# Spreading the tokens of experts 5 to 8 by transfers in SBUF and turning them on VectorE

## The chip, the core and the metric

One core of a Trainium2 chip runs the kernel. The core's engines work side by side, each through its own queue in order: PE (TensorE, matrix products), DVE (VectorE), ACT (ScalarE), POOL (GpSimd) and SP (SyncE, which here issues transfers). Products land in PSUM, from where DVE and ACT read them; everything else lies in SBUF. The metric is the device time of one execution in microseconds (us); lower is better, and a run is told by the median of its executions.

## The reference

Three stages follow each other. An attention stage makes 4352 tokens of 512 features, a dense layer with a softplus works on them, and then every token is given to one of eight experts, 544 tokens to each (`cap`), by the order of the gate's logits. The change touches only the last stage:

```python
def _moe2_ref(x, w_gate, w1, w2):
    ...
    out = np.zeros((N, D), dtype=np.float32)
    for e in range(E):
        mask = assigned == e
        h = np.maximum(x[mask] @ w1[e], 0.0)
        out[mask] = h @ w2[e]
    return out.astype(np.float32)
```

`x[mask]` is 544x512, `w1[e]` 512x1024, `w2[e]` 1024x512, all float32.

## The kernel before

All products of this stage are made from split operands: a value is kept as a high part (`hi`, rounded for the fast float32 product) and a low part (`lo`, the rest), and three products stand for one.

The loop over `ph` (line 1245) runs through the eight experts, `ph` 0 to 7, which the text calls experts 1 to 8. Each has two phases on PE. The **first phase** (line 1277) is 16 units of 12 products: `w1h`/`w1l` times the turned tokens `yTh`/`yTl`, a unit being one of eight slices of 128 hidden features by one of two parts of the tokens (`HALF`). From expert 2 on, the units begin with the part of tokens 256 to 543, which are pieces 2, 3 and 4, and take tokens 0 to 255, pieces 0 and 1, in the second unit. The **second phase** is a short block for the last 32 tokens (line 1308) and four blocks of 24 products (line 1322), for `a` = 2, 3, 0, 1. ACT copies the result of each block to `ot` (lines 1311 and 1328), and POOL scatters it to DRAM.

Between the matmuls of the second phase the next expert is prepared. `prepare` (line 1193) is a generator that is advanced 16 times, after every six products of the four blocks; each advance splits one eighth of `w1` (ACT copy, POOL difference, line 1158) and, when its condition holds, turns one piece of the tokens. `transposes` (line 1177) turns a piece of up to 128 tokens: four PE transposes of 128x128 into one PSUM bank `p_h` (of two), an ACT copy to `yTh` (line 1189), a DVE difference to `yTl` (line 1190). The tokens come to `xg` by five indirect gathers on POOL (line 1133). `load_w1` and `load_w2` bring the weights by one transfer of 2 MB each on SP.

Through the whole stage a third job runs in small steps at fixed places between the matmuls (`advance_route`, at the product numbers in `AT1`, `AT2` and `AT3`): it finds which tokens the next experts take. It is a chain that goes back and forth between DVE (lines 1019 to 1103) and short products on PE (lines 1044, 1061, 1072, 935, 940). It ends in the first phase of expert 6, so that the starts of experts 7 and 8 have none of it.

The order of the instructions on each engine is the order in which the program writes them; nothing reorders it later.

Of the kernel before, what the change touches and what calls it, by code (L numbers as in the profile page):

```python
# [8 lines left out]
F32 = mybir.dt.float32  # L9
# [21 lines left out]
def attn_moe_kernel(ctx, tc, x_s, x_t, state_t, w_in, w_out, w_gate, w1, w2, out):  # L31
    nc = tc.nc
    V, A, G, PE, SP = nc.vector, nc.scalar, nc.gpsimd, nc.tensor, nc.sync
# [7 lines left out]
    def bank(tag, bufs=1):  # L41
        return psum.tile([128, 512], F32, name="p_" + tag, tag=tag, bufs=bufs)
# [1062 lines left out]
    W1S, W2S, XG, W1, YT = {}, {}, {}, {}, {}  # L1105
    regs, gathered, unit = {}, {}, [0]

    def expert_reg(ph):
        if ph not in regs:
            regs[ph] = SP.value_load(RES[ph][0][0:1, 0:1], min_val=0, max_val=E - 1)  # L1110
        return regs[ph]

    def load_w1(ph):
        t = ldp.tile([128, 4, F2], F32, name="s1w")
        SP.dma_start(t, w1[bass.ds(expert_reg(ph), 1)].rearrange("o (k p) f -> p (o k) f", p=128))
        W1S[ph] = t

    def load_w2(ph):
        t = ldp.tile([128, 8, DM], F32, name="s2w")
        if ph == 0:  # L1120

            G.memset(t[0:1, 0, 0:1], 0.0)
        SP.dma_start(t, w2[bass.ds(expert_reg(ph), 1)].rearrange("o (k p) f -> p (o k) f", p=128))
        W2S[ph] = t

    def gather(ph, some=range(5)):
        idx = RES[ph][1]
        if 0 in some:
            XG[ph] = ldp.tile([128, 5, DM], F32, name="xg")
        xg = XG[ph]  # L1130
        for a in some:
            m = 128 if a < 4 else CAP - 512
            G.indirect_dma_start(out=xg[0:m, a, :], out_offset=None, in_=y_d[:, :],
                                 in_offset=bass.IndirectOffsetOnAxis(ap=idx[0:m, a:a + 1], axis=0))
        gathered[ph] = unit[0]

    def routing():
# [7 lines left out]
    for i, at_ in enumerate(route(0, False)):  # L1145
        if lazy and i % 2 == 0:
            lazy.pop(0)()
        rest(99 if at_ == "slots" else BETWEEN[i])
        if 0 in RES and 0 not in W1S:
            load_w1(0)  # L1150
# [4 lines left out]
    me = ctx.enter_context(tc.tile_pool(name="me", bufs=1))  # L1155
# [5 lines left out]
    def split_w1(ph, on=(G,)):  # L1161
        src = W1S.pop(ph)
        hi = w1p.tile([128, 4, F2], F32R, name="w1h")
        lo = w1p.tile([128, 4, F2], F32R, name="w1l")
        W1[ph] = (hi, lo)
        for i in range(8):
            c = slice(i * 128, (i + 1) * 128)
            split_piece(src[:, :, c], hi[:, :, c], lo[:, :, c], on[0])
            yield
# [7 lines left out]
    def transposes(ph):  # L1177
        xg = XG.pop(ph)
        hi = me.tile([128, 4, CAP], F32R, name="yTh")
        lo = me.tile([128, 4, CAP], F32R, name="yTl")  # L1180
        YT[ph] = (hi, lo)
        for a in range(5):
            m = 128 if a < 4 else CAP - 512
            p = bank("h", 2)
            for k in range(4):
                PE.transpose(p[:, k * m:(k + 1) * m], xg[0:m, a, k * 128:(k + 1) * 128], ident[0:m, 0:m])  # L1186
            src = p[:, 0:4 * m].rearrange("p (k c) -> p k c", k=4)
            c = slice(a * 128, a * 128 + m)
            A.activation(hi[:, :, c], src, AF.Copy)
            V.tensor_tensor(lo[:, :, c], src, hi[:, :, c].bitcast(F32), op=OP.subtract)  # L1190
            yield

    def prepare(ph):
        sp1, tr = split_w1(ph), transposes(ph)
        n = 0
        while True:
            a, b = next(sp1, 0), 1
            if unit[0] >= gathered[ph] + 12 or n > 8:
                b = next(tr, 0)
            n += 1  # L1200
            if a == 0 and b == 0:
                return
            yield
# [22 lines left out]
    W2_FROM = 5  # L1226
    on = [G]
    sp1, tr0 = split_w1(0, on), transposes(0)

    def begin(ops):  # L1230
        for op in ops:
            if op in "sv":
                on[0] = G if op == "s" else V
                next(sp1, 0)
            elif op == "t":
                next(tr0, 0)
            elif op == "r":
                advance_route()
            elif op == "x":
                gather(0, range(2))  # L1240
            else:
                gather(0, range(2, 5))
                load_w2(0)
    begin(BEGIN)
    for ph in range(E):
# [9 lines left out]
        def fetch():  # L1255
            q = ph + 1
            if q in RES and q not in W1S and q not in W1:
                load_w1(q)
            if q in RES and ph not in W2S and q not in W2S and sp2 is None:
                load_w2(q)  # L1260
            if len(RES.get(q, ())) == 2 and q not in XG and q not in YT:
                gather(q)

        evac = lambda: None
        for u in range(16):
            ft, hf = units[u] if ph else units0[u]
            f, c = slice(ft * 128, (ft + 1) * 128), HALF[hf]
            w = c.stop - c.start
            p = bank("h", 2) if u % 2 else bank("y2" if u % 4 else "y3")
            n = 0  # L1270
# [26 lines left out]
        for a in (4, 2, 3, 0, 1):  # L1297
            ot = me.tile([128, DM], F32, name="ot", bufs=3)
            p = bank(f"y{a % 2}" if a < 4 else "y1")
            if a == 4:  # L1300

                m, ws = TAIL, W2S.pop(ph)
                evac()
                for ft in range(8):
                    if ft in AT3:
                        advance_route()
                    for q in range(4):
                        PE.matmul(p[q * 32:(q + 1) * 32, 0:128], h2t[:, ft], ws[:, ft, q * 128:(q + 1) * 128],
                                  start=(ft == 0), stop=(ft == 7))
                for q in range(4):  # L1310
                    A.activation(ot[0:m, q * 128:(q + 1) * 128], p[q * 32:(q + 1) * 32, 0:128], AF.Copy)
                fetch()
            else:
                m = 128
                c = slice(a * 128, a * 128 + m)
                n = 0
                for ft in range(8):
                    fetch()
                    for l, r in ((h2h, w2h), (h2h, w2l), (h2l, w2h)):
                        if n in AT2:  # L1320
                            advance_route()
                        PE.matmul(p, l[:, ft, c], r[:, ft, :], start=(n == 0), stop=(n == 23))  # L1322
                        n += 1
                    if ft % 2 == 1:
                        if pre is None and ph + 1 in XG and ph + 1 in W1S:
                            pre = prepare(ph + 1)
                        advance(pre)
                A.activation(ot, p, AF.Copy)  # L1328
# [6 lines left out]
        if ph + 1 < E:  # L1335
            while ph + 1 not in YT or pre is None:
                advance_route()
                fetch()
                if pre is None and ph + 1 in XG and ph + 1 in W1S:
                    pre = prepare(ph + 1)  # L1340
                advance(pre)
            while advance(pre):
                pass
# [40 lines left out]
```

## Time and profile before

| | us |
|---|---|
| median of 3 runs | 1209.81 |
| lowest and highest run | 1209.26, 1211.1 |
| the profiled execution, its own time | 1206.22 |
| its span in the trace | 1204.4 |
| first unit of experts 5, 6, 7, 8 begins on PE at | 985.63, 1042.59, 1096.67, 1147.11 |

The profiled execution is 3.6 us under the median, and 1.8 us of its own time lie outside its span. The engines' busy shares are means over stages that differ; what a change in the last stage is worth is read from that stage. In the timeline every row is one or more instructions: start, duration, engine, line, operation, names and shape, count, and in brackets how long the engine had been idle before and what it waited for.

### The profile page before, as it was taken

What the parts mean: (1) busy time and instruction counts of PE and PEld (TensorE: products, weight loads), DVE (VectorE), ACT (ScalarE), POOL (GpSimd) and SP (SyncE); (2) the same over time, 40 slices, a digit from 0 to 9 for tenths busy, and PEclk for the clock granted to TensorE, in tenths of its full rate; (3) what the DMA queues carried; (4) which work ended last, traced back from release to release, by engine and by line L of the source; (5) the groups of instructions that cost most, each with busy time, mean ns of one, the idle gap of its engine ahead of it and who ended that gap; (6) DMA issues with size and microseconds to landing.
All of it is one profiled execution on the core that took longest, in us unless ns stands there. A gap on an engine that the chain in (4) does not pass through costs nothing.

```text
span 1204.4 us, 21169 instructions
## 1 busy us (share of the span) xinstructions
PE 1148.3 (95%) x8256; PEld 905.3 (75%) x8256; DVE 649.8 (54%) x1744; ACT 640.6 (53%) x1277; POOL 484.4 (40%) x472
## 2 busy tenths in 40 slices
PE   4798999999999999999999997999999999999996
PEld 1566677777677777777777765979797988889895
DVE  6998435463363533634434266776685767641120
ACT  3776666666676666766766732533333333343330
POOL 0333423232232232322344435645646555556531
PEclk9998999999999999999999999899999999999999
DMA  7454021111201201012000003250523425234201
GB/s 245 141 193 142 1 71 36 54 53 36 70 1 42 64 29 55 23 36 70 1 18 19 1 18 123 91 197 25 200 82 143 136 80 180 106 119 133 92 18 38
DMA packets 51060, 95.77 MB, mean 80 GB/s; under 512 B 4624, under 2 KB 19088, under 8 KB 50960
## 3 DMA queue, kind: packets, MB, share of 16 engines
q1 hardware_dynamic: 45232, 76.46, 19.4%
q0 software_dynamic: 5632, 17.83, 4.4%
q8 instruction: 65, 1.06, 0.4%
q14 instruction: 35, 0.29, 0.1%
q10 hardware_dynamic: 96, 0.13, 0.0%
HBM read 76.58 MB, written 17.83 MB: 78 GB/s over the span
## 4 chain that ended last, share of the span: by engine, by line
PE 79%; DVE 10%; issue 6%; POOL 2%; ACT 1%; DMA 1%; SPq 0%; POOLq 0%; DVEq 0%; ACTq 0%
PE p_h L491 13%; PE p_y L1322 12%; PE p_y L575 8%; PE p_y L577 8%; PE p_y L579 8%; PE p_y L1277 7%; PE p_h L1277 6%; PE p_bg L460 2%; PE p_y L582 2%; PE p_bg L502 2%; PE p_y L586 2%; PE p_y L584 2%; PE p_h L1186 1%; DVE c_a L198 1%; PE p_bg L1044 1%
## 5 line engine op out<-in xcount | busy, mean ns | idle before, releaser
L557 POOL TENSOR_TENSOR g_lo<-g,g_hi 128x512 fp32r<-128x512 f32 x127 | 164.1, 1293 | 324.6 <-ACT g_hi L554 268.1
L575 PE MATMUL p_y<-g_hi,wo_hi 128*128 128x512 f32 x448 | 185.6, 414 | 0.0
L577 PE MATMUL p_y<-g_hi,wo_lo 128*128 128x512 f32 x448 | 178.3, 398 | 3.6 <-POOL wo_lo L237 3.6
L579 PE MATMUL p_y<-g_lo,wo_hi 128*128 128x512 f32 x448 | 176.4, 394 | 0.0
L554 ACT ACTIVATE g_hi<-g 128x512 fp32r<-128x512 f32 x126 | 79.6, 632 | 118.5 <-DVE g L546 84.7
L546 DVE SCALAR_TENSOR_TENSOR g<-p_h,t_sp 128x512 f32<-128x512 f32 x128 | 87.5, 684 | 98.1 <-ACT t_sp L534 97.6
L575 PEld LDWEIGHTS p_y<-g_hi,wo_hi 128*128 128x128 f32 x448 | 85.1, 190 | 49.1 <-ACT t_sp L526 12.6
L1322 PE MATMUL p_y<-w2h,h2h 128*128 128x512 f32 x256 | 105.0, 410 | 0.0
L491 PE MATMUL p_h<-at_hi,P_hi 128*128 128x512 f32 x256 | 103.6, 405 | 1.4 <-DVE g L546 1.4
L491 PE MATMUL p_h<-at_hi,P_lo 128*128 128x512 f32 x256 | 101.6, 397 | 0.0
L491 PE MATMUL p_h<-at_lo,P_hi 128*128 128x512 f32 x256 | 101.5, 397 | 0.0
L1322 PE MATMUL p_y<-w2l,h2h 128*128 128x512 f32 x256 | 101.4, 396 | 0.0
L1322 PE MATMUL p_y<-w2h,h2l 128*128 128x512 f32 x256 | 101.2, 395 | 0.0
L577 PEld LDWEIGHTS p_y<-g_hi,wo_lo 128*128 128x128 f32 x448 | 85.3, 191 | 20.7 <-POOL wo_lo L237 4.9
L579 PEld LDWEIGHTS p_y<-g_lo,wo_hi 128*128 128x128 f32 x448 | 85.3, 190 | 19.4
L1330 POOL DMA_INDIRECT out_dram<-ot,idx x40 | 38.7, 969 | 143.8 <-ACT ot L1328 72.5
L526 ACT ACTIVATE t_sp<-p_h 128x512 f32<-128x512 f32 x128 | 75.4, 589 | 27.8 <-PE p_h L491 27.0
L1159 POOL TENSOR_TENSOR w2l<-s2w,w2h 128x512 fp32r<-128x512 f32 x64 | 81.6, 1291 | 13.1 <-ACT w2h L1158 12.3
L534 ACT ACTIVATE t_sp<-t_sp 128x512 f32<-128x512 f32 x128 | 80.9, 632 | 4.1
L1159 POOL TENSOR_TENSOR w1l<-s1w,w1h 128x512 fp32r<-128x512 f32 x63 | 80.1, 1297 | 6.0 <-ACT w1h L1158 5.2
L533 ACT ACTIVATE t_sp<-t_sp 128x512 f32<-128x512 f32 x128 | 80.7, 631 | 2.3
L1277 PE MATMUL p_y<-yTl,w1h 128*128 128x288 f32 (+1 forms) x256 | 77.3, 302 | 0.0
(282 smaller groups left out, 2611.0 us busy)
## 6 DMA issues: line engine op xcount, KB each, us to landing
s1w<-in_moe_w_dram SPq DMA_DIRECT2D x8, 2048.0 KB, 8.3
s2w<-in_moe_w_dram SPq DMA_DIRECT2D x8, 2048.0 KB, 9.1
st<-in_moe_w_in_dram SPq DMA_DIRECT2D x16, 512.0 KB, 4.1
xT<-in_x_t_dram SPq DMA_DIRECT2D x16, 512.0 KB, 4.4
st<-in_moe_w_out_dram SPq DMA_DIRECT2D x16, 512.0 KB, 3.8
xt<-in_x_s_dram SPq DMA_DIRECT2D x8, 1024.0 KB, 5.5
y_d<-yz SPq DMA_DIRECT2D x48, 128.0 KB, 3.5
y_d<-s_g SPq DMA_DIRECT2D x8, 128.0 KB, 2.5
```

The costliest lines, as they stand in the source:

```text
L491: PE.matmul(h, l[:, f0:f0 + 128], r[:, par, :], start=(n == 0), stop=(n == 5))
L533: A.activation(t, t, AF.Exp, scale=-1.0)
L534: A.activation(t, t, AF.Ln, bias=1.0)
L546: V.scalar_tensor_tensor(g[:, :w], hps.pop(s)[:, :w], 0.0, tsp.pop(s)[:, :w], op0=OP.max, op1=OP.add)
L554: A.activation(hi[:, c], g[:, c], AF.Copy)
L557: (G if on[1] == "G" else V).tensor_tensor(lo[:, c], g[:, c], hi[:, c].bitcast(F32), op=OP.subtract)
L575: PE.matmul(yb[j], wo_hi[:, ft, c], hi, start=st, stop=False)
L577: PE.matmul(yb[j], wo_lo[:, ft, c], hi, start=False, stop=False)
L579: PE.matmul(yb[j], wo_hi[:, ft, c], lo, start=False, stop=sp)
L1159: eng.tensor_tensor(lo, src, hi.bitcast(F32), op=OP.subtract)
L1277: PE.matmul(p[:, :w], l[:, k, f], r[:, k, c], start=(n == 0), stop=(n == 11))
L1322: PE.matmul(p, l[:, ft, c], r[:, ft, :], start=(n == 0), stop=(n == 23))
```

## The change

For experts 5 to 8 (`ph` from `TURNED` = 4 on) the tokens are no longer turned on PE. After the gather, 16 transfers on SP copy `xg` to a new tile `xz`, in pieces of 512 bytes, so that each partition block of 32 holds one quarter of the features of 32 tokens at a time. One DVE instruction per piece (`V.transpose`, which turns 32x32 blocks) then writes the turned piece to the PSUM bank that the four PE transposes filled before. The ACT copy and the DVE difference stay. The features come out in another order, so `w1` is loaded in that order, in four transfers of 32 partitions. The pieces are made in the order 2, 3, 4, 0, 1, and a turn is tried only from the advance with `n` above 12: three of the 16 advances, all in the block `a` = 1, the others after the last of them.

```diff
+    TURNED = 4
     def load_w1(ph):
         t = ldp.tile([128, 4, F2], F32, name="s1w")
-        SP.dma_start(t, w1[bass.ds(expert_reg(ph), 1)].rearrange("o (k p) f -> p (o k) f", p=128))
+        src = w1[bass.ds(expert_reg(ph), 1)]
+        if ph < TURNED:
+            SP.dma_start(t, src.rearrange("o (k p) f -> p (o k) f", p=128))
+        else:
+            for q in range(4):
+                SP.dma_start(t[q * 32:(q + 1) * 32], src[:, q * 128:(q + 1) * 128].rearrange("o (k c) f -> c (o k) f", c=32))
...
+        if ph >= TURNED:
+            xz = me.tile([128, 17, 128], F32, name="xz")
+            for a in range(4):
+                n = 5 if a == 0 else 4
+                for q in range(4):
+                    SP.dma_start(xz[q * 32:(q + 1) * 32, a::4], xg[a * 32:(a + 1) * 32, 0:n, q * 128:(q + 1) * 128])
+            XG[ph] = xz
         gathered[ph] = unit[0]
...
-        for a in range(5):
+        for a in (range(5) if ph < TURNED else (2, 3, 4, 0, 1)):
             m = 128 if a < 4 else CAP - 512
             p = bank("h", 2)
-            for k in range(4):
+            if ph >= TURNED:
+                V.transpose(p[:, 0:4 * m].rearrange("p (k t r) -> p t k r", k=4, r=32),
+                            xg[:, 4 * a:4 * a + m // 32].rearrange("p t (k c) -> p t k c", k=4))
+            for k in range(4 if ph < TURNED else 0):
                 PE.transpose(p[:, k * m:(k + 1) * m], xg[0:m, a, k * 128:(k + 1) * 128], ident[0:m, 0:m])
...
-            if unit[0] >= gathered[ph] + 12 or n > 8:
+            if unit[0] >= gathered[ph] + 12 and ph < TURNED or n > (8 if ph < TURNED else 12):
                 b = next(tr, 0)
```

On DVE, at the end of expert 4's second phase, the queue before holds only the chain of the routing (`pe`, `sat`, `df`, `mk`), and then the first results of expert 5 (`h2l`):

```order
L1039 SCALAR_TENSOR_TENSOR p_bg_6890<-df,p_bg_6890 128x1
L1049 SCALAR_TENSOR_TENSOR pe<-p_bg_10607,rem_6897 15x8
L1051 SCALAR_TENSOR_TENSOR pe<-p_bg_10607,pe 15x8 x2
L1052 TENSOR_TENSOR sat_6910<-p_bg_10607,pe 15x8
L1058 TENSOR_TENSOR p_bg_6890<-pat,p_bg_6890 128x16
L1063 TENSOR_REDUCE df<-p_bg_10630 128x1
L1026 SCALAR_TENSOR_TENSOR p_bg_6890<-df,p_bg_6890 128x16
L1031 TENSOR_TENSOR mk_6906<-v,p_bg_6890 128x34x16
```

In the changed kernel the same stretch of DVE's queue, from the first turn to the last, reads (the rows from L1026 to L1039 stand between `df` and the third turn in both):

```order
L1202 STREAM_TRANSPOSE p_h<-xz 128x4x4x32
L1209 TENSOR_TENSOR yTl<-p_h,yTh 128x4x128
L1049 SCALAR_TENSOR_TENSOR pe<-p_bg_10596,rem_6897 15x8
L1051 SCALAR_TENSOR_TENSOR pe<-p_bg_10596,pe 15x8 x2
L1052 TENSOR_TENSOR sat_6910<-p_bg_10596,pe 15x8
L1058 TENSOR_TENSOR p_bg_6890<-pat,p_bg_6890 128x16
L1202 STREAM_TRANSPOSE p_h<-xz 128x4x4x32
L1209 TENSOR_TENSOR yTl<-p_h,yTh 128x4x128
L1063 TENSOR_REDUCE df<-p_bg_10623 128x1
```

Two turns came in between the steps of the chain. A little further on DVE, after the chain's next `mk`, stand the other three:

```order
L1039 SCALAR_TENSOR_TENSOR p_bg_6890<-df,p_bg_6890 128x1
L1202 STREAM_TRANSPOSE p_h<-xz 128x128
L1209 TENSOR_TENSOR yTl<-p_h,yTh 128x4x32
L1202 STREAM_TRANSPOSE p_h<-xz 128x4x4x32
L1209 TENSOR_TENSOR yTl<-p_h,yTh 128x4x128
L1202 STREAM_TRANSPOSE p_h<-xz 128x4x4x32
L1209 TENSOR_TENSOR yTl<-p_h,yTh 128x4x128
```

Ten instructions came in, a turn and a difference for each piece, and the differences that stood in the blocks `a` = 2 and 3 before are now here.

On ACT, the same place before, from the copy of block `a` = 0 over that of block `a` = 1 to expert 5's first result:

```order
L1328 ACTIVATE ot<-p_y_10519 128x512
L1328 ACTIVATE ot<-p_y_10587 128x512
L1158 ACTIVATE w2h<-s2w 128x512
L1282 ACTIVATE h2h<-p_y_10652 128x256
L1158 ACTIVATE w2h<-s2w 128x512
```

And now:

```order
L1347 ACTIVATE ot<-p_y_10502 128x512
L1208 ACTIVATE yTh<-p_h 128x4x128 x2
L1208 ACTIVATE yTh<-p_h 128x4x32
L1347 ACTIVATE ot<-p_y_10570 128x512
L1208 ACTIVATE yTh<-p_h 128x4x128 x2
L1174 ACTIVATE w2h<-s2w 128x512
L1301 ACTIVATE h2h<-p_y_10657 128x256
```

The five copies to `yTh` moved from the blocks `a` = 2 and 3 to here: three behind the copy of block `a` = 0, two behind that of block `a` = 1.

## Rows read from the trace of the kernel before

**Rows 1.** Page: busy time of each engine, share of the span, instructions.

```profile
PE 1148.3 (95%) x8256; PEld 905.3 (75%) x8256; DVE 649.8 (54%) x1744; ACT 640.6 (53%) x1277; POOL 484.4 (40%) x472
```

**Rows 2.** Timeline, ACT: first and last copy of experts 7 and 8's second phases.

```profile
1122.77 1.11 ACT L1311 ACTIVATE ot<-p_y 32x128 f32<-32x128 f32 x4 [1.58 <-PE p_y L1308]
...
1147.19 0.60 ACT L1328 ACTIVATE ot<-p_y 128x512 f32<-128x512 f32 x1 [4.84 <-PE p_y L1322]
...
1173.20 1.11 ACT L1311 ACTIVATE ot<-p_y 32x128 f32<-32x128 f32 x4 [1.58 <-PE p_y L1308]
...
1195.16 0.60 ACT L1328 ACTIVATE ot<-p_y 128x512 f32<-128x512 f32 x1 [4.84 <-PE p_y L1322]
```

**Rows 3.** Groups by line: busy us, mean ns of one, idle before.

```profile
L1186 PE MATMUL p_h<-ident,xg 128*128 128x128 f32 (+1 forms) x160 | 24.1, 275 | 3.3 <-DMA xg<-y_d,idx 3.3
L284 DVE TENSOR_TENSOR Z<-Z,m 128x512 f32<-128x512 f32 x12 | 14.9, 1245 | 0.4
```

**Rows 4.** One tile's or line's instructions: least, median, greatest ns.

```profile
L282 DVE STREAM_TRANSPOSE Z<-ST x12: 700/701/703, 188.2 to 566.1; 128x512 f32<-128x512 f32 x12
L1189 ACT ACTIVATE yTh<-p_h x40: 277/598/602, 752.5 to 1131.9; 128x512 fp32r<-128x512 f32 x32, 128x128 fp32r<-128x128 f32 x8
L1190 DVE TENSOR_TENSOR yTl<-p_h,yTh x40: 291/691/693, 753.1 to 1132.3; 128x512 fp32r<-128x512 f32 x32, 128x128 fp32r<-128x128 f32 x8
```

**Rows 5.** Timeline at the start of expert 5, DVE and PE.

```profile
981.60 0.17 DVE L1039 SCALAR_TENSOR_TENSOR p_bg<-df,p_bg 128x1 int32<-128x1 int32 x1
...
982.86 0.17 DVE L1049 SCALAR_TENSOR_TENSOR pe<-p_bg,rem 15x8 f32<-15x8 f32 x1 [1.09 <-PE p_bg L1044]
...
983.53 0.15 DVE L1058 TENSOR_TENSOR p_bg<-pat,p_bg 128x16 int32<-128x16 int32 x1
...
984.58 0.17 DVE L1063 TENSOR_REDUCE df<-p_bg 128x1 f32<-128x8 f32 x1 [0.90 <-PE p_bg L1061]
...
985.63 0.30 PE L1277 MATMUL p_y<-yTh,w1h 128*128 128x288 f32 x1
...
986.19 0.16 DVE L1039 SCALAR_TENSOR_TENSOR p_bg<-df,p_bg 128x1 int32<-128x1 int32 x1
...
987.55 0.27 PE L1277 MATMUL p_h<-yTh,w1h 128*128 128x256 f32 x1
```

**Rows 6.** Timeline at the start of expert 6, DVE and PE.

```profile
1039.49 0.17 DVE L1063 TENSOR_REDUCE df<-p_bg 128x1 f32<-128x8 f32 x1 [0.28 <-PE p_bg L1061]
...
1041.55 0.17 DVE L1073 TENSOR_SCALAR p_bg<-p_bg 128x8 f32<-128x8 f32 x1 [1.44 <-PE p_bg L1072]
...
1042.59 0.29 PE L1277 MATMUL p_y<-yTh,w1h 128*128 128x288 f32 x1
...
1043.29 0.24 DVE L1087 SCALAR_TENSOR_TENSOR M<-cu,em,p_bg 128x34 bf16<-128x34 f32 x1
...
1044.47 0.36 PE L1277 MATMUL p_h<-yTh,w1h 128*128 128x256 f32 x1
```

**Rows 7.** Timeline, ACT, at the start of expert 7.

```profile
1096.75 0.60 ACT L1328 ACTIVATE ot<-p_y 128x512 f32<-128x512 f32 x1 [4.84 <-PE p_y L1322]
```

**Rows 8.** Chain that ended last (start us, us): expert 7's first unit.

```profile
1096.67 1.60 PE p_y L1277 x12
```

**Rows 9.** Timeline, PE: a wait of PE between two matmuls.

```profile
114.41 0.80 PE L577 MATMUL p_y<-g_hi,wo_lo 128*128 128x512 f32 x1 [2.15 <-POOL wo_lo L237]
```

**Rows 10.** Two stretches: length, busy us by engine, granted clock, DMA share, GB/s.

```profile
112.00:116.00 4.00, 1.85 (x6) 1.30 (x5) 3.96 (x8) 2.64 (x6) 3.60 (x2) 0.80 0.86 290
116.00:120.00 4.00, 4.00 (x18) 3.22 (x17) 2.80 (x6) 0.95 (x3) 0.00 (x0) 0.77 0.03 10
```

**Rows 11.** Transfers: issues, KB each, median us from issue to landing.

```profile
y_d<-yz SPq DMA_DIRECT2D x48, 128.0 KB, 3.5
xg<-y_d,idx POOLq DMA_INDIRECT x40, 3.8
```

**Rows 12.** Timeline, POOL: the last of expert 5's five gathers.

```profile
957.48 0.88 POOL L1133 DMA_INDIRECT xg<-y_d,idx  x1 [0.30 <-issue]
```

## The prediction

> **What bounds the kernel now.** I read the page's busy times first: TensorE is busy for 95% of the span [rows 1]. Then the timeline at the starts of experts 5 to 8: the first unit follows the last block of the expert before without a wait, and the second unit follows the first [rows 5, 6, 8]. So in this stage PE ends last everywhere, work taken from its stream is worth its full length, and any new wait at a start costs its full length too. The chain that ended last says the same: a whole unit of expert 7 stands on it as twelve matmuls in a row [rows 8].
>
> **What the change removes.** Four PE transposes per piece, 20 per expert, 80 in all, and they lie in PE's stream. Their price is read from two second phases that differ in nothing else: expert 7's holds the transposes for expert 8, expert 8's holds none, and neither has a routing step. From the first copy behind the short block to the copy of the last block it is 1147.19 - 1122.77 = 24.42 us with them and 1195.16 - 1173.20 = 21.96 us without [rows 2]. So 2.46 us per expert, 0.49 us per group of four, and 4 x 2.46 = **9.8 us gained**. PE's routing waits in these phases are short, so experts 5 and 6 get the same value.
>
> The transposes' own mean duration is 275 ns [rows 3], which would make 80 of them 22 us; but four of them overlap, as the 0.49 us shows, and the step counts. The Trainium skill (VectorE: DVE Perf Modes, "The three transpose paths" and "Rules for kernel authors") speaks against this change: for a 128x128 transpose it says to use TensorE where PSUM is a good place for the result, at 390 ns against 311 ns on VectorE (bf16). By its 390 ns the sum would gain 31 us in place of 9.8 and end near 1204; the step of 0.12 us in this trace disagrees with that figure, and agrees with the rule.
>
> **What it adds, off the path.** 16 transfers per expert of some 68 KB in 512-byte pieces. SP sends them when the gather is in: for expert 5 the last gather ends at 958.4 and lands some 3.8 us later [rows 11, 12], so they start near 962. A transfer of 128 KB in 512-byte pieces lands in 3.5 us [rows 11]; even one after another 16 take under 56 us, but they are queued together and hold 1.1 MB, 9 of those 128 KB. I take 10 to 15 us, to 977 at the latest; the first turn comes near 982, so nothing waits. Behind them on SP stands only the load of `w2` of the same expert, which is needed after 986 and took 9 us; `w1` in four transfers has 25 us to spare. I cost both at nothing; if that cover failed at expert 5, each us of lateness there would be a us of the time.
>
> **What it adds, on the path.** A turn of 128x512 takes 0.70 us on DVE, the ACT copy 0.60, the DVE difference 0.69; the short piece some 0.3 for each [rows 4]. Into PSUM no row shows a turn: the ends are 0.60 (ACT over the same 512 columns) and 1.25 (the slowest two-operand DVE operation of this size [rows 3]); I take 0.70, as DVE's reads of PSUM cost 0.69. For each hand-over between engines I allow 0.05 us. What decides is the order. On DVE a difference waits for its ACT copy, and the next turn stands behind that difference: a piece is 0.70 + 0.60 + 0.69 and three hand-overs, about 2.1 us, with no overlap between pieces. On ACT the copies of pieces 2, 3 and 4 stand behind the copy of block `a` = 0, those of 0 and 1 behind that of block `a` = 1, which waits for PE's last product. Before, all this lay 25 us earlier.
>
> *Start of expert 5*, times from PE's old start 985.63 [rows 5]. DVE is through with L1039 at -3.9. Piece 2: turn to -3.1, copy to -2.5, difference to -1.7. Then the routing's L1049 to L1058 (0.82 us from 982.86 to 983.68), which used to run at -2.8; `sat` comes at -1.0, where PE's L1061 wants it by -1.2: PE is 0.3 late. Piece 3: -0.9 to 1.2. Then L1063 to L1039 (984.58 to 986.35, 1.8 us) to 3.0. Piece 4: turn 3.3, copy 3.6, difference 3.95, and only then has the first unit its operands: PE stands still from 0.3 to 3.6 and has its second matmul at 4.0. Piece 0: 4.0 to 6.1. Piece 1: turn 6.8, copy 7.45, difference 8.2. The second unit, which began at 987.55 (+1.9), gets going at 8.2 where it had its second matmul at 2.0: **6.2 us late**.
>
> *Start of expert 6*, from 1042.59 [rows 6]. DVE is free at 1039.21, -3.4 (the row's 0.28 us of idling). Piece 2 to -1.3. L1063 and the two short ones behind it, 0.6, to -0.7; PE's L1072, which ran by -1.2, waits for them, about 1.0. Piece 3 to 1.5. L1073 to L1087 (1041.55 to 1043.53, 2.0 us) to 3.5. Piece 4 to 4.45, piece 0 to 6.6, piece 1 to 8.7. Behind that stands the routing's `tot`, for which PE's L940 waits ahead of the second unit: 9.05 in place of +1.88: **7.2 us late**.
>
> *Starts of experts 7 and 8* have no routing. ACT is through with block `a` = 0 at -4.8 (4.84 us of idling ahead of the row at 1096.75, [rows 7]), the first turn is long done, and pieces 2, 3 and 4 end at -0.3: the first unit doesn't wait. ACT copies block `a` = 1 from 0.1 to 0.7. Piece 0: copy 1.3, difference 2.05. Piece 1: turn 2.75, copy 3.4, difference 4.15. The second unit is due at 1.6 [rows 8] and has its second matmul at 4.2 in place of 1.7: **2.5 us late**, twice.
>
> Together 6.2 + 7.2 + 2.5 + 2.5 = **18.4 us lost**.
>
> **The clock.** After a wait of 2.15 us PE's granted clock fell: its mean was 0.80 and then 0.77 in two stretches of 4 us, parts of which ran at 1.2 in place of 2.4 GHz [rows 9, 10]. That is 4 x 0.20 + 4 x 0.23 = 1.7 us of work lost, behind the wait and on top of it. Two other waits, of 1.87 and 2.13 us, show the same pattern. The new waits are of this kind: 3.3 us and again 1.7 us at experts 5 and 6, 2.5 us at 7 and 8 broken by one matmul. Four falls at 1.7 are **6.9 us**; the ends are 0 and, with a second fall at experts 5 and 6, 10.3.
>
> **The sum.** 18.4 + 6.9 - 9.8 = +15.5 us. The profiled execution would go from 1206.2 to 1221.7; the median of the runs stands 3.6 above it, and 1209.8 + 15.5 = **1225**. A turn of 0.60 takes off 12 x 0.1 (twelve serial turns: four each at experts 5 and 6, two each at 7 and 8) = 1.2; one of 1.25 adds 12 x 0.55 = 6.6. The forecast's own range is 1220 to 1230.
>
> **Rivals.**
> - *Waits without the clock*: the waits are cut by single units and the clock stays at 2.4 GHz. 1209.8 + 18.4 - 9.8 = 1218. For it: at experts 7 and 8 one matmul breaks the wait. Against: the three waits of about 2 us in this trace that were all followed by 1.2 GHz.
> - *Turns slow or transfers late*: a turn into PSUM costs 1.25 us, or the transfers for expert 5 come after 982. 1225 + 6.6 = 1232. For it: no row shows such a turn, and the transfers of 32 partitions are new. Against: reads of PSUM cost no more than those of SBUF here, and there are some 5 us to spare.
> - *Faster: the waits stay under what PE saves.* PE gains 2.46 us per expert; if the last piece is done that soon after the first unit, the change wins. This mechanism sits at experts 7 and 8, where 2.5 late against 2.46 is already even, and would have to hold at 5 and 6 too; with no wait at all it gives 1209.8 - 9.8 = 1200. It decides at 9.8 us of waits in all, with the clock held. For it: DVE does little besides in experts 7 and 8. Against: the order on DVE and ACT is fixed, and the chain for pieces 0 and 1 alone is 3.5 us behind ACT's last copy.
> - *The transposes are worth their durations* (22 us, by 275 ns each): 1209.8 + 25.3 - 22 = 1213. Against: the two second phases above, which differ by 2.46 us and not by 5.5.
>
> **Chances.** Forecast 0.50, waits without the clock 0.22, slow turns or late transfers 0.10, transposes worth more 0.05, faster 0.09; the remaining 0.04 is a loss and gain that cancel. A measurement of this kernel can tell 0.2% (2.4 us) from no change: faster 0.10, same 0.05, slower 0.85. The range leaves out the faster and the cancelled cases, and part of the slowest: 1214 to 1232.
>
> **What would show it.** Right: L1202 at 0.70 us; PE idle before L1296 `p_y` for some 3 us at experts 5 and 6, released by ACT or DVE on `yTh`/`yTl`; idle before L1296 `p_h` at all four starts; granted clock under 1 in the 4 us behind each; second phases of experts 4 to 7 shorter by 2.4 us. Wrong: a first turn released by a transfer, turns far from 0.70, second units that follow the first without a wait, or a clock of 1.00 throughout.

## The result and the profile after

The changed kernel takes 1224.3 us (median of 5 runs, 1223.2 to 1224.6) where the kernel before took 1210.85 beside it: a ratio of 1.0112, 95% interval [1.0097, 1.0126]. It is 13.5 us slower; the prediction was 1225.0, slower. A later group of runs, with before 5.0 and the changed kernel 6.5 us faster, gave 1205.88 for before and 1217.85 for the changed kernel, a ratio of 1.0096 [1.0081, 1.0112].

The page of the changed kernel, its span and busy times, which answer to [rows 1]: the 80 transposes are gone from PE's count, DVE has 20 instructions more, and the span is 18.3 us longer than before's.

```profile
span 1222.7 us, 21159 instructions
...
PE 1152.8 (94%) x8176; PEld 907.6 (74%) x8176; DVE 660.6 (54%) x1764; ACT 640.2 (52%) x1277; POOL 485.6 (40%) x472
```

The waits of PE from 975 us to the end (engine, line, what it waited for: total us, times, longest):

```profile
PE p_y L1296 <- ACT yTh L1208: 5.4, 2, 2.8
PE p_h L1296 <- ACT yTh L1208: 3.5, 3, 1.6
...
PE p_bg L940 <- DVE tot L937: 0.8, 1, 0.8
...
PE p_h L1296 <- DVE yTl L1209: 0.7, 2, 0.3
```

Before, PE had no wait on `yTh` or `yTl` at any start. Now there are two of 2.8 and 2.6 us ahead of the first units of experts 5 and 6, and one or two ahead of the second units of experts 5, 7 and 8; ahead of expert 6's second unit PE waits for the routing's `tot` (L940). The start of expert 5, ACT, DVE and one weight load of PE (PEld; start us, us, instruction, and in brackets the idle time ahead with what ended it):

```profile
990.32 0.59 ACT L1347 ACTIVATE ot<-p_y 128x512 f32<-128x512 f32 x1
...
990.45 0.29 DVE L1209 TENSOR_TENSOR yTl<-p_h,yTh 128x128 fp32r<-128x128 f32 x1 [0.34 <-ACT yTh L1208]
...
990.47 0.19 PEld L1296 LDWEIGHTS p_y<-yTh,w1h 128*128 128x128 f32 x1 [3.25 <-ACT yTh L1208]
...
990.66 0.72 DVE L1202 STREAM_TRANSPOSE p_h<-xz 128x512 f32<-128x512 f32 x1
...
991.41 0.60 ACT L1208 ACTIVATE yTh<-p_h 128x512 fp32r<-128x512 f32 x1 [0.50 <-DVE p_h L1202]
...
992.04 0.69 DVE L1209 TENSOR_TENSOR yTl<-p_h,yTh 128x512 fp32r<-128x512 f32 x1 [0.66 <-ACT yTh L1208]
...
992.65 0.72 DVE L1202 STREAM_TRANSPOSE p_h<-xz 128x512 f32<-128x512 f32 x1
...
993.40 0.60 ACT L1208 ACTIVATE yTh<-p_h 128x512 fp32r<-128x512 f32 x1 [1.39 <-DVE p_h L1202]
...
994.03 0.69 DVE L1209 TENSOR_TENSOR yTl<-p_h,yTh 128x512 fp32r<-128x512 f32 x1 [0.66 <-ACT yTh L1208]
```

This is the chain that the prediction wrote down: turn, copy, difference, and only then the next turn; from 990.66 to 992.65 it is 1.99 us for a piece. PE stands until the copy of the short piece, at 990.47, and the second unit has its second operand (`yTl` of the last piece) only at 994.7.

**Where the time went.** In a table by stage I count from the first output copy of a short block to that of the next expert's: one second phase, in which PE is spared the transposes, and one first phase with its start. To keep both kernels comparable I take the second profile of each (taken in the experiments, spans 1204.2 and 1216.1 us); below them stand the other kernels, described in the next section. All but the first line are differences from before, in us. (The first profile lost 2.4 us more ahead of this table, in expert 4's short block.) The two copies of the last column (expert 8) in the changed kernel's second profile, 52.00 us apart; for before, [rows 2] shows the same two in its first profile, 50.43 apart as well:

```profile
1132.90 1.11 ACT L1330 ACTIVATE ot<-p_y 32x128 f32<-32x128 f32 x4 [1.58 <-PE p_y L1327]
...
1184.90 1.11 ACT L1330 ACTIVATE ot<-p_y 32x128 f32<-32x128 f32 x4 [1.58 <-PE p_y L1327]
```

| | start of expert 5 | 6 | 7 | 8 | sum |
|---|---|---|---|---|---|
| before, length | 56.36 | 56.89 | 50.44 | 50.43 | 214.12 |
| changed, second profile | +5.30 | +3.38 | +1.54 | +1.57 | +11.8 |
| changed, first profile | +7.20 | +5.54 | +1.55 | +1.56 | +15.9 |
| PE transposes, late | +0.95 | +0.18 | +0.19 | +0.20 | +1.5 |
| waits filled | +3.65 | +3.40 | +0.02 | +0.04 | +7.1 |
| turn ahead of difference | +1.75 | +0.28 | -1.37 | -1.35 | -0.7 |
| early turns | +2.81 | +6.26 | -2.48 | -2.46 | +4.1 |
| early and ahead | -0.32 | +1.95 | -2.48 | -2.46 | -3.3 |
| experts 7, 8 alone, early | +0.06 | -0.04 | -2.48 | -2.46 | -4.9 |
| experts 7, 8 alone, late | +0.01 | -0.06 | +1.53 | +0.05 | +1.5 |

Each changed column holds a saving of 2.46, so the starts of the changed kernel (second profile) cost 7.76, 5.84, 4.00 and 4.03. The saving is measured at experts 7 and 8 and taken over for 5 and 6; there PE comes to the first unit 1.8 and 1.3 us sooner than before, counted from the first copy, or 2.2 each without its waits for the routing on the way.

### The profile page after: what moved, and what is told of

Read it like the earlier page. It is cut to its first block, busy times and chain, and to the rows that moved or that the text cites. A ratio compares the mean times of both kernels' runs of the same rounds, so it can differ in the third digit from the quotient of the medians.

```text
span 1222.7 us, 21159 instructions
## 1 busy us (share of the span) xinstructions
PE 1152.8 (94%) x8176; PEld 907.6 (74%) x8176; DVE 660.6 (54%) x1764; ACT 640.2 (52%) x1277; POOL 485.6 (40%) x472
## 4 chain that ended last, share of the span: by engine, by line
PE 77%; DVE 11%; issue 6%; ACT 2%; POOL 2%; DMA 1%; another core or an unknown queue 0%; SPq 0%; POOLq 0%; DVEq 0%; ACTq 0%
PE p_h L491 13%; PE p_y L1341 11%; PE p_y L575 8%; PE p_y L577 8%; PE p_y L579 8%; PE p_y L1296 7%; PE p_h L1296 7%; PE p_bg L460 2%; PE p_bg L502 2%; PE p_y L582 2%; PE p_y L586 2%; PE p_y L584 2%; DVE c_a L198 1%; DMA st<-in_moe_w_in_dram 1%; PE p_y L1327 1%
## 5 line engine op out<-in xcount | busy, mean ns | idle before, releaser
L1296 PE MATMUL p_y<-yTh,w1h 128*128 128x288 f32 (+1 forms) x256 | 79.9, 312 | 5.4 <-ACT yTh L1208 5.4
```

What stands on the lines that cost most here:

```text
L1296: PE.matmul(p[:, :w], l[:, k, f], r[:, k, c], start=(n == 0), stop=(n == 11))
```

## Experiments

### The loss is not in the transfers

```diff
+        for q in range(4 if ph >= 4 else 1):
...
+        if ph >= 4:
+            xz = me.tile([128, 17, 128], F32, name="xz")
...
+                    SP.dma_start(xz[q * 32:(q + 1) * 32, a::4], xg[a * 32:(a + 1) * 32, 0:n, q * 128:(q + 1) * 128])
```

> The kernel before plus the transfers of the change alone: 16 transfers of 512-byte rows for each of experts 5 to 8 into a tile that nobody reads, and w1 of these experts in four transfers; PE transposes as before. Theory A: they lie beside other work, within 1.5 us of 1210.85. Rival B (the transfers take the time, by holding back the gathers, the weights or the scatters behind them): 5 us or more above it.

`w1` comes here in four transfers too, but in its old order. Measured: 1205.98 us against 1206.68, ratio 0.9997 [0.9988, 1.0007]. The transfers cost nothing that can be measured, as the prediction had it.

### Lateness alone is nearly free

```diff
-        for a in range(5):
+        for a in (range(5) if ph < 4 else (2, 3, 4, 0, 1)):
...
-            if unit[0] >= gathered[ph] + 12 or n > 8:
+            if unit[0] >= gathered[ph] + 12 and ph < 4 or n > (8 if ph < 4 else 12):
```

> The kernel before with the other half of the change alone: experts 5 to 8 still turn their tokens by PE transposes, but from the 13th piece on, in the order 2, 3, 4, 0, 1; no turns on VectorE, no transfers, w1 in one transfer. Theory A (lateness): the last two pieces stand behind the second phase, and PE waits there for a chain without the 0.70 of the turn on VectorE: after the last matmul of the phase 2 x 0.49 of transposes, the output copy 0.60, two copies of 0.60 and a difference of 0.69, of which the first unit (1.5 us) covers part: 1 to 1.5 us of wait at each start, up to 1 more before the first unit of experts 5 and 6, and up to 1.7 us of lower clock at each: 4 to 12 us above before, 1215 to 1223. Rival B (the turns on VectorE and the transfers are the cost): within 2 us of 1210.85.

Measured: 1207.48, ratio 1.0009 [1.0000, 1.0018], far under the 4 to 12 us that were expected of lateness. At the start of expert 7, PE and ACT:

```profile
1096.10 1.78 PE L1186 MATMUL p_h<-ident,xg 32*128 32x32 f32 x12
...
1096.74 0.59 ACT L1328 ACTIVATE ot<-p_y 128x512 f32<-128x512 f32 x1
...
1097.21 1.30 ACT L1189 ACTIVATE yTh<-p_h 128x512 fp32r<-128x512 f32 x2
...
1097.63 0.38 PE L1277 MATMUL p_y<-yTh,w1h 128*128 128x288 f32 x1
```

The last transposes run straight behind the last product; both copies follow the output copy back to back (1.30 us for two), and the first unit covers them. What was left out of the expectation is that PE turns the last piece without waiting for the difference of the one before. So the late place alone does not lose the time; the turns that share VectorE's queue with the differences have to come with it.

### The chain in VectorE's queue

```diff
+        turned = turn(2) if ph >= TURNED else None
...
             A.activation(hi[:, :, c], src, AF.Copy)
+            if ph >= TURNED and a != 1:
+                turned = turn({2: 3, 3: 4, 4: 0, 0: 1}[a])
             V.tensor_tensor(lo[:, :, c], src, hi[:, :, c].bitcast(F32), op=OP.subtract)
```

> The changed kernel with one thing moved: each turn on VectorE stands ahead of the difference of the piece before it instead of behind it, so that it runs while ScalarE copies; the pieces still start from the 13th. Theory A (what makes the starts late is the serial chain of turn 0.70, copy 0.60, difference 0.69 in VectorE's queue, 2.0 us a piece): a piece comes every 1.4 us at experts 5 and 6 (four steps, 2.4 us less of wait each), at 7 and 8 the turn of the last piece is done before the output copy and some 1.4 us of the 2.3 go; 7.6 us less of waits and 2 to 5 of the lower clock: 8 to 13 us under the changed kernel of this group, near before. Theory B (the place in the program alone decides, not the chain on VectorE): within 2 us of it.

Measured: 1206.65, ratio to before 1.0004 [0.9995, 1.0014]; the changed kernel beside it 1217.85. So 11.2 us of the 12.0 go, by moving one instruction in one engine's queue: each turn now stands ahead of the difference of the piece before, and with that also ahead of the routing steps that stood between two pieces at experts 5 and 6. The start of expert 5 now, DVE and ACT:

```profile
985.07 0.72 DVE L1201 STREAM_TRANSPOSE p_h<-xz 128x512 f32<-128x512 f32 x1
...
985.82 0.60 ACT L1212 ACTIVATE yTh<-p_h 128x512 fp32r<-128x512 f32 x1 [1.02 <-DVE p_h L1201]
...
986.00 0.73 DVE L1201 STREAM_TRANSPOSE p_h<-xz 128x512 f32<-128x512 f32 x1
...
986.63 1.45 DVE L1215 TENSOR_TENSOR yTl<-p_h,yTh 128x512 fp32r<-128x512 f32 x2
```

The turns of the last two pieces start 0.93 us apart instead of 1.99, inside ScalarE's copies. At experts 7 and 8, where no routing step is in the way, the table shows 1.37 and 1.35 us gained where 1.54 and 1.57 were lost. The starts are not free, though: with the saving of 2.46 counted in each column they still cost 4.2, 2.7, 1.1 and 1.1 us, 9.1 in all, where they cost 21.6 in the changed kernel.

### The clock behind the waits

```diff
+            for _ in range({4: (22, 12), 5: (22, 12), 6: (0, 12), 7: (0, 12)}.get(ph, (0, 0))[u] if u < 2 else 0):
+                PE.matmul(p[:, :w], w1h[:, 0, f], w1h[:, 0, 0:w], start=True, stop=True)
```

> The changed kernel with matrix products put into PE's waits at the starts of experts 5 to 8: ahead of the first unit 22 products of the weights with themselves (experts 5 and 6), ahead of the second unit 12 (all four); the unit's own first product then starts its sum anew, so that nothing of them is left. They are put so as to end no later than the waits do. Theory A (the lower clock behind the starts, 7.1 us in all, is what PE's waits bring with them): the clock stays at full behind the starts, the waits themselves stay as long, and the time falls by 4 to 7 us against the changed kernel of this group. Theory B (the clock falls whatever PE does there, or the time at the lower clock is hidden by waits that follow): within 1.5 us of it, or above by the added products.

Measured: 1213.62 against 1217.85, 4.2 us less. Stretches of the changed kernel's second profile behind the start of expert 7, and of the filled kernel's (busy us by engine with instructions, then the granted clock, DMA share, GB/s):

```profile
core 0: us, PE busy (x) PEld busy (x) DVE busy (x) ACT busy (x) POOL busy (x), PEclk, DMA share, GB/s
1104.00:1108.00 4.00, 2.04 (x13) 1.61 (x13) 2.53 (x5) 1.91 (x4) 2.03 (x3) 0.94 0.71 226
1108.00:1112.00 4.00, 4.00 (x23) 4.00 (x23) 0.56 (x2) 1.46 (x4) 3.09 (x4) 0.63 0.48 121
```

```profile
1104.00:1108.00 4.00, 3.51 (x27) 3.31 (x28) 2.11 (x5) 2.00 (x5) 2.01 (x3) 1.00 0.61 208
1108.00:1112.00 4.00, 4.00 (x34) 4.00 (x33) 1.37 (x4) 2.63 (x6) 3.08 (x4) 1.00 0.48 138
```

The clock is 0.94 and 0.63 in the one and 1.00 in the other, while the wait itself stays: from the output copy to the second product of expert 7's second unit it is 25.81 us in both. By the table the start of expert 5 costs 1.65 less, those of 7 and 8 1.52 and 1.53 less, and that of expert 6 nothing less. There the fall lies in front of another wait, for the routing's `tot` (L940), which came at the same distance either way. So theory A holds for three starts, and theory B's second half (hidden by a wait that follows) for one.

### Experts 7 and 8 alone, late

```diff
-    TURNED = 4
+    TURNED = 6
```

> The change for experts 7 and 8 alone, late as in the change (from the 13th piece, turns behind differences); experts 5 and 6 as in the kernel before. Against the kernel with the same two experts turned from the 9th piece (0.9966 of before) only the place differs. Theory A (the losses of the four experts add up, and at 7 and 8 there is no routing in them): from the times between output copies, a start of these two costs 4.0 and saves 2.46, so 2 x 1.55 = 3.1 us above before, 1.0026 (1.001 to 1.004). Theory B (the loss at 7 and 8 follows from what was late at 5 and 6): at or below before.

Measured: 1207.62 against 1206.72, 1.0009 [1.0000, 1.0018], less than the 1.0026 expected; the interval begins at no change. The profile says why. Expert 7's second unit and expert 8's wait equally long:

```profile
1097.88 0.38 PE L1296 MATMUL p_h<-yTh,w1h 128*128 128x256 f32 x1 [1.62 <-ACT yTh L1208]
...
1149.86 0.38 PE L1296 MATMUL p_h<-yTh,w1h 128*128 128x256 f32 x1 [1.62 <-ACT yTh L1208]
```

but the granted clock behind them differs (the same columns as above):

```profile
1097.00:1101.00 4.00, 2.78 (x12) 2.58 (x13) 1.41 (x4) 1.91 (x4) 2.28 (x2) 0.70 0.42 164
1101.00:1105.00 4.00, 4.00 (x30) 4.00 (x30) 0.95 (x3) 2.08 (x5) 2.93 (x4) 0.87 0.63 174
1149.00:1153.00 4.00, 2.80 (x20) 2.61 (x21) 1.77 (x5) 2.71 (x6) 2.54 (x2) 1.00 0.17 66
1153.00:1157.00 4.00, 4.00 (x34) 4.00 (x33) 0.99 (x4) 2.11 (x6) 3.42 (x3) 1.00 0.00 0
```

Behind the first it is 0.70 and 0.87, behind the second 1.00. The waits alone cost what the transposes save (2.5 each), so what is left is the clock's, 1.53 at the one start and 0.05 at the other in the table; over ten runs the time went from 1206.1 to 1209.0. The losses of the starts add up, with the clock's part left to vary.

### Early turns, and what they push aside

```diff
-            if unit[0] >= gathered[ph] + 12 and ph < TURNED or n > (8 if ph < TURNED else 12):
+            if unit[0] >= gathered[ph] + 12 and ph < TURNED or n > 8:
```

> The changed kernel with one number undone: the turns of experts 5 to 8 start from the 9th piece of the preparation (n over 8) as in the kernel before, everything else of the change stays (turns on VectorE, transfers, w1 in four, order 2, 3, 4, 0, 1). Theory A (the cost is lateness: turns from the 13th piece end after the second phase, PE waits 17 us at four starts and loses 7 us more at the lower clock): all five pieces are ready before the second phase ends, no wait of PE over 0.6 us at the starts, no clock fall there, and what is left is the saving of 4 x 2.46 = 9.8: 1201 us (1199 to 1205). Rival B (the turns themselves, their copies or the transfers cost the time, whenever they run): it stays at 1218 or more. Rival C (the turns get in the way of routing on VectorE or of copies on ScalarE when they run earlier): between, 1205 to 1215, with new waits inside the second phases.

Measured: 1210.49, 1.0030 [1.0018, 1.0042] against 1206.68: none of the gain arrived in the sum, and theory A as stated fell. PE begins the first two units of each of the four experts without a wait, and experts 7 and 8 gain 2.48 and 2.46; but the phases ahead of experts 5 and 6 lose. Ahead of expert 6, DVE and PE:

```profile
1041.97 0.71 DVE L1202 STREAM_TRANSPOSE p_h<-xz 128x512 f32<-128x512 f32 x1
...
1043.35 0.69 DVE L1209 TENSOR_TENSOR yTl<-p_h,yTh 128x512 fp32r<-128x512 f32 x1 [0.66 <-ACT yTh L1208]
...
1044.07 0.17 DVE L1049 SCALAR_TENSOR_TENSOR pe<-p_bg,rem 17x8 f32<-17x8 f32 x1
...
1044.75 0.14 DVE L1054 TENSOR_TENSOR pel<-p_bg,pe 17x8 f32<-17x8 f32 x1
...
1044.95 0.19 PE L1061 MATMUL p_bg<-sat,taken 128*128 128x8 bf16 x1 [2.70 <-DVE pel L1054]
```

The routing's steps from L1049 to L1054 stand in VectorE's queue behind the turn of piece 0, and behind a difference that itself waits 0.66 us for ScalarE; PE's L1061 waits 2.70 us for them, with the second phase's products queued behind it. This is rival C of the expectation.

The same with the turns ahead of the differences:

```diff
+            if ph >= TURNED and a != 1:
+                turned = turn({2: 3, 3: 4, 4: 0, 0: 1}[a])
...
+            if unit[0] >= gathered[ph] + 12 and ph < TURNED or n > 8:
```

> Both moves at once on the changed kernel: all four experts' turns from the 9th piece on, and each turn ahead of the difference of the piece before it. With early turns alone PE waited 0.7, 1.3 and 2.6 us in the phase ahead of expert 5 and 0.8, 0.8 and 2.7 ahead of expert 6 for routing steps, and in VectorE's rows each difference ahead of those steps waited 0.64 to 0.67 us for ScalarE's copy. Theory A (VectorE holds the routing back by waiting in its queue as well as by working): the waits of four pieces go at each of the two experts, 4 x 0.65 = 2.6 each, 5.2 us less than with early turns alone (1.003): about 0.5 us under before, and still 4 above the kernel that turns experts 7 and 8 alone. Theory B (it is VectorE's work alone that holds the routing back, 2 x 3.2 us of turns): within 1.5 us of early turns alone, 3 to 4 us above before.

This kernel joins the two edits, the early turns and the turn ahead of the difference. Measured: 1202.97 against 1206.72, 0.9972 [0.9961, 0.9983], 3.75 us under before; 0.5 had been expected. By the table it loses 3.1 and 4.3 us less than early turns alone at experts 5 and 6, against 2.6 each by the count of VectorE's own waits. From 930 us on, PE's waits on the routing's `sat` and `pel` fell from 7.7 to 3.3 us in all, in the waits of the kernel with early turns alone

```profile
PE p_bg L1061 <- DVE sat L1052: 5.0, 4, 2.6
PE p_bg L1061 <- DVE pel L1054: 2.7, 1, 2.7
```

and in those of the kernel with both:

```profile
PE p_bg L1061 <- DVE pel L1054: 1.7, 1, 1.7
PE p_bg L1061 <- DVE sat L1052: 1.6, 3, 0.8
```

So VectorE holds the routing back by its waits at least as much as by its work. At expert 5 PE's waits alone account for the 3.1: they are 3.3 us shorter. At expert 6 they are 1.7 shorter ahead of the first unit, and the clock adds to it. Behind the waits of 2.70 us (early turns alone) and of 1.73 us (both), two stretches of each kernel (columns as above):

```profile
1044.00:1048.00 4.00, 3.05 (x8) 2.48 (x9) 2.54 (x11) 0.60 (x1) 0.00 (x0) 0.51 0.17 66
1048.00:1052.00 4.00, 4.00 (x19) 3.46 (x18) 1.81 (x11) 0.73 (x2) 0.00 (x0) 0.64 0.00 0
```

```profile
1036.00:1040.00 4.00, 2.27 (x17) 1.64 (x17) 3.76 (x14) 1.20 (x2) 0.36 (x2) 0.91 0.19 70
1040.00:1044.00 4.00, 4.00 (x15) 3.27 (x14) 1.13 (x6) 0.00 (x0) 0.00 (x0) 0.66 0.00 0
```

From that L1061 to the first unit PE runs without another wait, but takes 6.07 us in the one and 4.92 in the other, where it took 3.35 before. So the clock behind that wait costs 2.7 us with early turns alone and 1.6 with both, 1.1 less, and the rest lies in expert 6's first phase (30.77 us against 29.52).

### Turns where VectorE is free

```diff
-    TURNED = 4
+    TURNED = 6
...
-            if unit[0] >= gathered[ph] + 12 and ph < TURNED or n > (8 if ph < TURNED else 12):
+            if unit[0] >= gathered[ph] + 12 and ph < TURNED or n > 8:
```

> Turns on VectorE for experts 7 and 8 alone (2.46 us of PE's transposes saved at each), from the 9th piece on; experts 5 and 6 as in the kernel before. In the kernel with early turns for all four, PE waited 7.5 us in the phases ahead of experts 5 and 6 for routing steps that stood behind turns in VectorE's queue, and nowhere for experts 7 and 8, where routing is over. Theory A (the early turns cost only what they hold back of routing): 2 x 2.46 = 4.9 us under before, at 1201.8 where before is at 1206.7 (1200.5 to 1203). Theory B (something else of the turns costs as much): within 1.5 us of before or above it.

Measured: 1201.32 against 1205.88, 0.9966 [0.9952, 0.9979]. Its output copies from the first behind the short block to the last, in expert 6's second phase, which prepares expert 7, answer to [rows 2]:

```profile
1072.02 1.11 ACT L1330 ACTIVATE ot<-p_y 32x128 f32<-32x128 f32 x4 [1.58 <-PE p_y L1327]
...
1093.97 0.60 ACT L1347 ACTIVATE ot<-p_y 128x512 f32<-128x512 f32 x1 [2.37 <-PE p_y L1341]
```

1093.97 - 1072.02 = 21.95 us, where before it was 24.42 with the transposes and 21.96 without; the first phase behind it is 26.01 as before. This kernel is 4.6 us faster than the one before and 16.5 faster than the changed one beside it; it and the kernel with early turns ahead of their differences are the only ones clearly below before.

### Second profiles of both kernels, unchanged

> The kernel before, unchanged, for a second profile. In the profile of the changed kernel PE lost some 2.4 us ahead of the short block of expert 4 in waits that no semaphore ended, and 1.4 us more at a lower clock right behind, in code that the change does not touch; the profile of before has neither, and its run (1206.2) was 4.6 us under its median. Theory A1 (such a loss belongs to most executions of either kernel, and the first profile of before was one without it): this profile's run is near 1210 and has a loss of 2 us or more at that place. Theory A2 (the loss came with the change): no such loss here.

Before's second profile has a span of 1204.2 us (its run 1205.96) and no loss at expert 4's short block, so theory A1 is not borne out.

> The changed kernel, unchanged, as the base of this group. By its first ratio (1.0112) it stands 13.5 us above before, at 1220.2 where before is at 1206.7. What is open is the 3.8 us that its first profile lost in and behind the short block of expert 4 (PE waits of 1.06 and 0.59 us that no semaphore ended, then 4 us at a lower clock), which neither profile of before has, nor that of the kernel with early turns. Theory A (an accident of that one execution): no such waits in this profile, its span 3 to 4 us nearer to before's. Theory B (it belongs to the change): the same waits at the same instructions.

Nor has the changed kernel's: the loss came neither with each execution nor with the change (theory A). PE in the short block of expert 4, first in the first profile of the changed kernel:

```profile
958.08 0.38 PE L1327 MATMUL p_y<-s2w,h2t 128*32 128x128 f32 x3 [0.59 <-issue]
...
959.52 0.66 PE L1327 MATMUL p_y<-s2w,h2t 128*32 128x128 f32 x13 [1.06 <-issue]
```

and in the second, where 40 products follow each other without a gap:

```profile
956.57 1.30 PE L1327 MATMUL p_y<-s2w,h2t 128*32 128x128 f32 x40
```

So the 3.8 us at that place (2.4 ahead of the copy of the short block, 1.4 behind it) belong to that execution and not to the change. A second difference is at the start of expert 6, where both profiles have the same wait ahead of the first unit (2.56 and 2.55 us), but the clock stays low for a different time, first profile and then second (columns as above):

```profile
1052.00:1056.00 4.00, 2.44 (x10) 2.34 (x11) 2.92 (x11) 1.36 (x3) 0.97 (x1) 0.61 0.29 70
1056.00:1060.00 4.00, 3.19 (x16) 2.98 (x16) 3.17 (x13) 1.91 (x4) 2.31 (x2) 0.50 1.02 214
1060.00:1064.00 4.00, 4.00 (x23) 4.00 (x22) 3.93 (x10) 1.31 (x4) 1.48 (x2) 0.61 1.04 272
```

```profile
1049.00:1053.00 4.00, 3.55 (x13) 3.14 (x14) 2.51 (x5) 2.11 (x5) 0.97 (x1) 0.57 0.66 155
1053.00:1057.00 4.00, 3.45 (x29) 3.45 (x29) 3.76 (x17) 2.01 (x6) 3.23 (x3) 1.00 1.02 262
```

In the first profile that is 4 x (0.39 + 0.50 + 0.39) / 0.5 = 10.2 us at the lower level (1.2 in place of 2.4 GHz), in the second 4 x 0.43 / 0.5 = 3.4. The longer fall outlasts the wait for `tot` and costs 2.2 us more (34.04 against 31.89 for the phase). Of the 6.6 us between the two spans (1222.7 and 1216.1) the two places explain 6.0. Why before was 4.6 us longer too in that group of runs than in its profiles is open: no profile of such a run of it exists.

## Why the prediction was right, and where it was not

The direction and the time came out (1225.0 forecast, 1224.3 measured, range 1214 to 1232). That the two lie only 0.7 apart is luck in part: the prediction set out from 1209.81 and added 15.5, while before measured 1210.85 beside the changed kernel, which is 13.5 above it, and 12.0 in the later group. By its steps:

- **What the transposes are worth, 2.46 us per expert: right.** Where nothing else moves, the kernel with experts 7 and 8 alone, the stages are 2.48 and 2.46 shorter. The sign that it named for it came out at two of four places: the second phases that prepare experts 7 and 8 are 2.46 us shorter by their output copies, those that prepare experts 5 and 6 are 0.8 and 1.0 longer, since PE waits there for routing steps and the last output copy stands behind copies to `yTh`. The rival that prices them by their 275 ns is refuted, and so is the one in which the waits stay under what PE saves: no start cost less than 4.0.
- **The turn at 0.70: right.** All twenty, changed kernel, least, median and greatest ns:

```profile
L1202 DVE STREAM_TRANSPOSE p_h<-xz x20: 317/717/730, 983.3 to 1163.1; 128x512 f32<-128x512 f32 x16, 128x128 f32<-128x128 f32 x4
```

- **Transfers at nothing: right** (0.9997), though SP spends some 0.6 us on each of the 64, about 10 us per expert, more than the prediction spoke of. One turn, the first of expert 7, waits 4.4 us for its transfer and still is ready long before ScalarE comes to copy it.
- **Starts of experts 7 and 8, 2.5 us late each: right.** They cost 4.00 and 4.03, of which 1.52 and 1.53 go with the clock; 2.5 each is left.
- **Start of expert 5, 6.2 late: right**, 7.76 less the clock's 1.65 is 6.1.
- **Start of expert 6, 7.2 late: too much.** The second profile has 5.84, and nothing of it goes with the clock. At the second matmul of the second unit PE is 6.15 late: 0.85 from its wait at L1072 and 5.3 behind that. The prediction let the routing's `tot` come 1 us later than it did, by small allowances at each step (a piece takes 1.99 us where 2.1 were allowed); and two waits for the routing further on became 0.2 us shorter each. PE's idle time ahead of this second unit stands before L940 and not before L1296, as the prediction's sign had it for all four starts.
- **The clock, 6.9 us: right in kind, too regular.** The first profile had falls behind all four starts; in the second the falls cost 1.65, 0, 1.52 and 1.53, 4.7 in all, since the one at expert 6 lay ahead of a wait. As four equal terms it was mis-sized; the rival without the clock (1218) was not right either: the filled kernel, whose clock stays at 1.00 behind the starts, is 7.7 us above before and the changed one beside it 12.0.

The sum by the second profiles is -9.8 + 16.9 + 4.7 = +11.8 where +15.5 was forecast. The medians differ by 13.5 us in the first group of runs, whose profile has the longer falls, and by 12.0 in the second. The step that was off is the start of expert 6 with its clock term: 3.1 us of the 3.7 between the two sums.

**Why it loses: the prediction's chain, with its two parts told apart.** The prediction has a serial chain and a late place. Late pieces turned by PE cost 0.8 us, so the late place alone does not do it. Late turns on VectorE put ahead of the differences also end within 1 us of before (0.8 above by the runs, 0.7 below by the table), but there the 9.8 us that PE saves pay for starts that still cost 9.1. The other 11.2 us are the order: a turn standing behind the difference of the piece before, which stands behind ScalarE's copy, at a place with no cover. Nor is the late place the only bad one: early turns push routing steps back at experts 5 and 6, which the prediction had not looked at.

The Trainium skill (VectorE: DVE Perf Modes, "Rules for kernel authors") says to turn 128x128 blocks on TensorE where PSUM will do for the result. With VectorE still busy with routing the runs agree in the main (none of the five kernels that turned expert 6 on VectorE had its column shorter than before, and for expert 5 one had, by 0.3 us); at experts 7 and 8, where PE is the bound and VectorE has no routing to do, they don't: the kernel that turns these two early is at 0.9966. The Trainium skill's 390 ns per transpose (VectorE: DVE Perf Modes, "The three transpose paths", bf16), by which the prediction's other sum ended near 1204, is not borne out by a saving of 2.48 us for twenty.

## What to carry to other kernels

Taking work from the engine that is the bound pays its full step (here 2.46 us per expert) only if the engine that takes it over has nothing in its queue that the bound waits for; look at what stands behind each added instruction, and at what the instruction ahead of it waits for. In an in-order queue put the instruction that starts the next piece ahead of the one that waits for the last: here that move alone was worth 11 us. Count a wait of the matmul engine as possibly dearer than its length, and don't count on it.

## What the runs showed of the hardware

The lower clock behind a wait was not the same from place to place: a wait of 1.62 us was followed by a granted clock of 0.70 and then 0.87 over stretches of 4 us at expert 7, and by 1.00 at expert 8 in the same execution; in the kernel with early turns a wait of 2.62 us ahead of expert 5 was followed by 1.00 (988 to 992 us), and one of 2.70 us ahead of expert 6 by 0.51 and 0.64; waits of 2.56 and 2.55 us at the same instruction were followed by 10.2 us and by 3.4 us at the lower level. The Trainium skill (TensorE: Matmul & The Clock Gate, "Part 1: The HAM clock gate (the "warmup" mystery)") says of the products at a kernel's start that how many of them run at the lower clock differs from run to run of the same kernel; these rows show the same behind a wait. And 34 matrix products that nobody needs, put into the two waits of expert 5's start, held the clock at 1.00 and gave back 1.65 us there.
